# Moving the zero fills from GpSimd's DMA queue to SyncE's, and the loads and stores the other way

One core of one Trainium2 chip. The metric is the device time of one execution in microseconds; medians of several executions are quoted.

## The reference

The outputs are one forward value and eight gradients of a block made of one query's attention and a gated feed-forward layer, all bf16.

```python
# x: (1,1,448); k_cache, v_cache: (1, 8, 32768, 256); wq: (448, 4096); wo: (4096, 448)
# w_gate, w_up: (448, 1792); w_down: (1792, 448)
W = 4096                                     # only the last 4096 of 32768 keys are used
q = (layernorm(x) @ wq)                      # 16 heads of 256, two for each of 8 key heads
p = softmax(q @ k_cache[:, :, Sk-W:].T / 16)
h = x + (p @ v_cache[:, :, Sk-W:]) @ wo
g, u = layernorm(h) @ w_gate, layernorm(h) @ w_up
out = h + (g * u) @ w_down
# returned: out and the gradients by x, k_cache, v_cache, wq, wo, w_gate, w_up, w_down
```

What matters here is the size of two of the gradients. Those by `k_cache` and `v_cache` have 134 MB each, and seven eighths of each are zero, because only the last 4096 rows of a head are used. So 235 MB of zeros have to be written, out of 335 MB that the kernel moves.

## The kernel before

A zero tile of 128 rows by 16 KB in on-chip memory is the source of nearly all fills. One fill writes it to 2 MB of `out_2` or `out_3` in 128 rows. Its upper half is lent to feed-forward weights for a while, so there are three groups: 42 full fills, 13 that read the lower half twice ("half fills", rows of 8 KB), and, once VectorE has zeroed the upper half again, 48 more full ones. Five late jobs write the last 18.9 MB from another region.

```python
LD = nc.sync                                 # loads and stores
ZQ = nc.gpsimd                               # zero fills
HALF0, HALF1 = 42, 55
...
LD.dma_start(out=wqA, in_=wq_A)              # query weights, 3.67 MB in two pieces
LD.dma_start(out=wqB, in_=wq_B)
LD.dma_start(out=x_bf[:], in_=A_x.rearrange("a b d -> (a b) d"))
...
def send_fills(n0, n1, halves=False):
    for reg in fills[n0:n1]:
        if halves:                           # L131
            ZQ.dma_start(out=reg.rearrange("p (k f) -> p k f", k=2), in_=zeros[:, 0:ZW // 2].unsqueeze(1).to_broadcast([128, 2, ZW // 2]))
        else:                                # L133
            ZQ.dma_start(out=reg, in_=zeros)

send_fills(0, HALF0)
send_fills(HALF0, HALF1, True)
...
load_kv(K_off[0], A_k_cache, 0)              # L197: a head's keys or values, 2 MB
LD.dma_start(out=dh2_bc[:], in_=grad_out.rearrange("a b d -> (a b) d").to_broadcast([128, D]))   # L200
...
if n == 1:                                   # in the feed-forward backward
    nc.vector.memset(ar(ZW // 2, ZW // 2), 0.0)      # L433: the second zeroing
    send_fills(HALF1, len(fills))
...
LD.dma_start(out=wq2A, in_=wq_A)             # L461: the query weights once more
LD.dma_start(out=wq2B, in_=wq_B)             # L462
...
for o, g, n0, n1, f in late_jobs:            # L663: 18.9 MB of zeros
    reg = zero_rows(o, g, n0, n1, f)
    for i in range(reg.shape[0]):
        LD.dma_start(out=reg[i], in_=ar(2 * ZW - f, f))
```

The source order is not the order of issue: a scheduler sorts the instructions of each engine when the program is built, and on one queue they are then issued strictly in that order. SyncE's and ScalarE's transfers go over what the profile calls the hardware path, GpSimd's over the software path.

Of the kernel before, what the change touches and what calls it, by code (L numbers as in the profile page):

```python
# [24 lines left out]
EPS = 1e-5  # L25
SCALE = 1.0 / 16.0
ZW = 8192
HALF0, HALF1 = 42, 55
NZ = (Sk - W) * Dh // (128 * ZW)
KB = 512  # L30

# [2 lines left out]
def kernel(  # L34
        ctx, tc, A_x, A_k_cache, A_v_cache, A_wq, A_wo, B_x, B_w_gate, B_w_up, B_w_down, grad_out,
           out_0, out_1, out_2, out_3, out_4, out_5, out_6, out_7, out_8):
    nc = tc.nc
    LD = nc.sync
    ZQ = nc.gpsimd

    const = ctx.enter_context(tc.tile_pool(name="const", bufs=1))
    small = ctx.enter_context(tc.tile_pool(name="small", bufs=2))
# [11 lines left out]
    def ar(off, n):  # L54
        return arena[:, off:off + n]

    def kv_at(off):
        return ar(off, T * Dh).rearrange("p (t d) -> p t d", d=Dh)
# [6 lines left out]
    wqA = ar(MB, 24 * KB).rearrange("p (c j) -> p c j", c=3)  # L65
    wqB = ar(MB + 24 * KB, 4 * KB)
# [29 lines left out]
    x_bf = const.tile([1, D], bf16)  # L96
    dh2_bc = const.tile([128, D], bf16)
    wq_A = A_wq[0:384, :].rearrange("(c p) j -> p c j", c=3)
    wq_B = A_wq[384:D, :].rearrange("r (h j) -> (r h) j", h=2)
    LD.dma_start(out=wqA, in_=wq_A)  # L100
    LD.dma_start(out=wqB, in_=wq_B)
    LD.dma_start(out=x_bf[:], in_=A_x.rearrange("a b d -> (a b) d"))

    ident_bf = const.tile([128, 128], bf16)
    make_identity(nc, ident_bf[:])
# [9 lines left out]
    def zero_rows(o, g, n0, n1, f):  # L115
        reg = o[0, g, 0:Sk - W, :].rearrange("s d -> (s d)")[n0 * 128 * ZW:n1 * 128 * ZW]
        return reg.rearrange("(n p f) -> n p f", p=128, f=f)
# [3 lines left out]
    for g in range(G):  # L121
        for o in (out_2, out_3):
            if g == G - 1 and o is out_3:
                continue
            reg = zero_rows(o, g, 0, 5 if g == G - 1 else NZ, ZW)
            fills += [reg[i] for i in range(reg.shape[0])]
# [8 lines that stand above are left out]
# [61 lines left out]
    def load_kv(off, cache, g):  # L196
        LD.dma_start(out=kv_at(off), in_=cache[0, g, Sk - W:, :].rearrange("(p t) d -> p t d", t=T))  # L197

    load_kv(K_off[0], A_k_cache, 0)
    LD.dma_start(out=dh2_bc[:], in_=grad_out.rearrange("a b d -> (a b) d").to_broadcast([128, D]))  # L200
    load_kv(V_off[0], A_v_cache, 0)
# [61 lines left out]
    with tc.tile_pool(name="ps_m", bufs=1, space=bass.MemoryType.PSUM) as ps_m, \  # L263
# [61 lines left out]
        def load_wo(n):  # L325
            LD.dma_start(out=wo_sb[:, 16 * n:16 * n + 16, :], in_=A_wo.rearrange("(p j) n -> p j n", j=32)[:, 16 * n:16 * n + 16, :])

# [18 lines left out]
    def block_views(n):  # L346
        f0, nb = BLOCKS[n]
        w = 128 * nb
        wgu = ar(wgu_off[n % 2], 8 * w).rearrange("p (c i f) -> p c i f", c=4, i=2)
        wd = ar(wd_off[n % 2], nb * D).rearrange("p (b n) -> p b n", n=D)  # L350
        return f0, nb, w, wgu, wd

    def load_block(n):
        f0, nb, w, wgu, wd = block_views(n)
        for eng, i, wt in ((LD, 0, B_w_gate), (nc.scalar, 1, B_w_up)):
            eng.dma_start(out=wgu[:, 0:3, i, :], in_=wt[0:384, :].rearrange("(c p) f -> p c f", c=3)[:, :, f0:f0 + w])
            eng.dma_start(out=wgu[0:DQ, 3, i, :], in_=wt[384:D, f0:f0 + w])
        LD.dma_start(out=wd, in_=B_w_down[f0:f0 + w, :].rearrange("(p b) n -> p b n", b=nb))

    load_block(0)  # L360
    load_block(1)

    with tc.tile_pool(name="ps_mid", bufs=3, space=bass.MemoryType.PSUM) as ps_mid, \
# [34 lines left out]
        for n in range(len(BLOCKS)):  # L398
# [31 lines left out]
            if n + 2 < len(BLOCKS):  # L430
                load_block(n + 2)
# [63 lines left out]
    with tc.tile_pool(name="work2", bufs=2) as work2, tc.tile_pool(name="lnw", bufs=1) as lnw, \  # L495
# [164 lines left out]
        for o, g, n0, n1, f in late_jobs:  # L660
            reg = zero_rows(o, g, n0, n1, f)
            for i in range(reg.shape[0]):
                LD.dma_start(out=reg[i], in_=ar(2 * ZW - f, f))  # L663

# [1 line left out]
_INS = ['A_x', 'A_k_cache', 'A_v_cache', 'A_wq', 'A_wo', 'B_x', 'B_w_gate', 'B_w_up', 'B_w_down', 'grad_out']  # L666
# [26 lines left out]
```

## Time and profile before

| | before |
|---|---|
| time, median (range) of 4 runs | 798.87 us (798.55 to 799.08) |
| span of the profiled run | 797.2 us |
| bytes moved, mean rate | 334.76 MB, 420 GB/s |
| busy: TensorE, VectorE, ScalarE | 60%, 55%, 25% |
| 334.76 MB at 431 GB/s (the good slices) | 776.7 us |

Whatever the kernel takes beyond 776.7 us is time in which the 16 DMA engines were not all at work at their best. In any stretch of the span it is (431 - rate) x length / 431.

### The profile page before, as it was taken

How to read it: one execution, taken by the hardware profiler on the slowest of the kernel's cores; microseconds unless marked ns; L12 is line 12 of the kernel's file. 1: busy time of each engine (PE TensorE's matmuls, PEld its weight loads, DVE VectorE, ACT ScalarE, POOL GpSimd, SP SyncE). 2: the span in 40 equal slices, each digit the busy share in tenths (PEclk: the TensorE clock that was granted, in tenths of full speed). 3: DMA queues.
4: the chain of work that ended last, by engine and by line, in shares of the span. 5: the costliest groups of instructions: out<-in, count | busy, mean ns of one | idle time of the engine just before them, and what ended most of it. 6: DMA issues, size and time to landing. Idle time of an engine off the chain costs nothing.

```text
span 797.2 us, 7318 instructions
## 1 busy us (share of the span) xinstructions
PE 478.9 (60%) x2926; PEld 222.6 (28%) x2926; DVE 437.1 (55%) x629; ACT 196.0 (25%) x309; POOL 61.8 (8%) x112
## 2 busy tenths in 40 slices
PE   0459999999999999251409478684450553722000
PEld 0334434344344333121208334331220211310000
DVE  2116584765846782263690679579653784964000
ACT  0142314134132201010102126353330442534000
POOL 4000000010101111100210001010000000000000
PEclk9989999999999999555558779766555556765555
DMA  9999999999999999999999999999999999999995
GB/s 349 431 430 430 428 431 430 430 428 430 430 423 427 427 419 413 423 421 424 432 428 423 424 431 431 428 425 427 424 424 422 424 424 424 423 427 418 433 434 247
DMA packets 29352, 334.76 MB, mean 420 GB/s; under 512 B 2819, under 2 KB 5894, under 8 KB 7814
## 3 DMA queue, kind: packets, MB, share of 16 engines
q0 software_dynamic: 16496, 216.01, 64.0%
q1 hardware_dynamic: 11382, 116.68, 34.8%
q10 hardware_dynamic: 1440, 1.61, 0.6%
q8 instruction: 23, 0.38, 0.2%
q14 instruction: 11, 0.09, 0.0%
HBM read 53.69 MB, written 280.59 MB: 419 GB/s over the span
## 4 chain that ended last, share of the span: by engine, by line
PE 37%; DMA 32%; DVE 16%; ACT 4%; issue 2%; another core or an unknown queue 0%; SPq 0%; DVEq 0%; ACTq 0%
DMA out_dram<-arena 19%; PE M_ps L317 12%; PE ok_ps L320 7%; PE rows_ps L256 6%; PE tr_ps L253 4%; DMA dh_bc<-in_grad_out_dram 4%; DMA arena<-in_A_k_cache_dram 4%; DMA arena<-in_B_w_down_dram 3%; ACT arena L270 2%; DVE arena L635 2%; DVE arena L459 2%; PE dqb_ps L502 2%; DMA arena<-in_B_w_gate_dram 2%; DVE arena L650 2%; PE d_ps L643 2%
## 5 line engine op out<-in xcount | busy, mean ns | idle before, releaser
L312 DVE TENSOR_TENSOR arena<-arena,p_f 128x2048 bf16<-128x2048 bf16 x64 | 145.4, 2286 | 61.6 <-PE M_ps L317 61.5
L317 PE MATMUL M_ps<-arena 128*128 128x512 bf16 x512 | 128.9, 380 | 0.2 <-ACT arena L323 0.2
L643 PE MATMUL d_ps<-arena,rT 32*128 32x512 bf16 x256 | 46.6, 529 | 111.0 <-DVE arena L651 63.9
L253 PE MATMUL tr_ps<-ident_bf,arena 128*128 128x128 bf16 x1024 | 92.5, 242 | 19.6 <-ACT arena L611 11.2
L256 PE MATMUL rows_ps<-arena,vpad 128*16 128x512 bf16 x256 | 90.6, 451 | 19.9 <-DVE arena L613 14.6
L133 POOL DMA_DIRECT2D out_dram<-arena x90 | 48.6, 542 | 538.5 <-DMA out_dram<-arena 491.3
L253 PEld LDWEIGHTS <-arena 128*128 128x128 bf16 x1024 | 69.0, 108 | 73.8 <-issue 64.4
L270 ACT COPY arena<-tr_ps 128x1024 bf16<-128x1024 bf16 x64 | 61.8, 1015 | 64.7 <-PE tr_ps L253 64.7
L647 ACT CAST arena<-d_ps 128x512 bf16<-128x512 f32 x64 | 37.7, 589 | 128.4 <-PE d_ps L643 128.3
L320 PE MATMUL ok_ps<-arena 128*16 128x512 bf16 x256 | 63.8, 381 | 0.9 <-DVE arena L297 0.9
L317 PEld LDWEIGHTS <-arena 128*128 128x128 bf16 x512 | 43.3, 99 | 59.0 <-issue 23.2
L611 ACT COPY arena<-tr_ps 128x1024 bf16<-128x1024 bf16 x32 | 32.6, 1019 | 94.6 <-PE tr_ps L253 36.4
L650 DVE CAST arena<-d_ps 128x512 bf16<-128x512 f32 x64 | 43.8, 684 | 16.9 <-PE d_ps L643 16.4
L651 DVE CAST arena<-d_ps 128x512 bf16<-128x512 f32 x64 | 43.5, 679 | 11.2 <-DMA out_dram<-arena 11.2
L643 PEld LDWEIGHTS <-rT 32*128 32x128 bf16 x256 | 11.2, 96 | 136.5 <-issue 90.0
L648 ACT CAST arena<-d_ps 128x512 bf16<-128x512 f32 x64 | 38.1, 595 | 11.9 <-DMA out_dram<-arena 11.9
L635 DVE TENSOR_TENSOR arena<-R_sb,tl_f 128x4096 bf16<-128x4096 bf16 x8 | 35.4, 4419 | 0.7 <-ACT R_sb L633 0.7
L256 PEld LDWEIGHTS <-vpad 128*16 128x16 bf16 x256 | 19.1, 92 | 58.4 <-issue 51.3
L320 PEld LDWEIGHTS <-arena 128*16 128x16 bf16 x256 | 19.1, 89 | 41.6 <-issue 20.5
L514 DVE CUSTOM_DVE_ANT_0 arena<-arena 128x4096 bf16<-128x4096 bf16 x3 | 13.1, 4423 | 23.9 <-ACT arena L507 23.9
L285 ACT ACTIVATE e_f<-cols_ps,nbias 128x32 f32<-128x32 f32 x16 | 4.5, 286 | 86.8 <-DVE nbias L281 86.8
L258 DVE COPY arena<-rows_ps 16x512 f32<-16x512 f32 x16 | 10.8, 676 | 26.6 <-PE rows_ps L256 26.6
(198 smaller groups left out, 387.9 us busy)
## 6 DMA issues: line engine op xcount, KB each, us to landing
out_dram<-arena POOLq DMA_DIRECT2D x103, 2048.0 KB, 51.7
out_dram<-arena SPq DMA_DIRECT2D x18, 2048.0 KB, 32.3
arena<-in_A_v_cache_dram SPq DMA_DIRECT2D x10, 2048.0 KB, 50.0
arena<-in_A_k_cache_dram SPq DMA_DIRECT2D x8, 2048.0 KB, 29.2
out_dram<-arena SPq DMA_DIRECT2D x4, 4096.0 KB, 43.8
arena<-in_A_wq_dram SPq DMA_DIRECT2D x2, 3072.0 KB, 20.6
arena<-in_A_wo_dram SPq DMA_DIRECT2D x2, 1792.0 KB, 14.5
out_dram<-arena SPq DMA_DIRECT2D x2, 1792.0 KB, 15.1
```

The costliest lines, as they stand in the source:

```text
L133: ZQ.dma_start(out=reg, in_=zeros)
L253: nc.tensor.transpose(tr_ps[:, dh, i, :], X_sb[:, 4 * q + i, dh * 128:(dh + 1) * 128], ident_bf[:])
L256: nc.tensor.matmul(rows_ps[:], lhsT=pad[:, dh, 16 * q:16 * q + 16], rhs=XT[:, dh].rearrange("p t k -> p (t k)"), start=(q == 0 and dh == 0 ...
L270: sT_ps = dots(kv_at(K_off[g]), KT_slot, vpad[g % 2], rows1, ps_c, "cols", lambda q, XT, ps: nc.scalar.copy(out=XT, in_=ps))
L312: nc.vector.tensor_tensor(out=pK, in0=K_sb[:, 4 * c:4 * c + 4, :].unsqueeze(2).to_broadcast([128, 4, 2, Dh]), in1=p_f[:, c::8, :].unsqueez ...
L317: nc.tensor.matmul(M_ps[:, vh, :], lhsT=V_sb[:, t, vh * 128:(vh + 1) * 128], rhs=pK[:, i, :, :].rearrange("p h d -> p (h d)"), start=(t == ...
L320: nc.tensor.matmul(ok_ps[:].rearrange("p k d -> p (k d)"), lhsT=ppad[g % 2][:, 8 * (t % 4) + t // 4, :], rhs=both(g, t), start=(g == 0 and ...
L635: nc.vector.tensor_tensor(out=RB_, in0=R_sb[:].unsqueeze(1).to_broadcast([128, 8, 512]), in1=tl_f[:].unsqueeze(2).to_broadcast([128, 8, 51 ...
L643: nc.tensor.matmul(d_ps[:, qi].rearrange("p w d -> p (w d)"), lhsT=rT[32 * q:32 * (q + 1), :], rhs=RB_[32 * q:32 * (q + 1), l, :], start=T ...
L648: nc.scalar.copy(out=stK[:, t:t + 2, :], in_=d_ps[:, :, 1, :])
L650: nc.vector.tensor_copy(out=stV[:, t:t + 2, :], in_=d_ps[:, :, 0, :])
L651: nc.vector.tensor_copy(out=stK[:, t:t + 2, :], in_=d_ps[:, :, 1, :])
```

## The change

The intent: SyncE, which computes nothing, issues the long row of fills, and GpSimd no longer spends time writing their descriptors. The query weights' first load stays at the head of the queue that is ready first. HALF1 goes from 55 to 61 so that the fills last until the second zeroing.

```diff
-HALF0, HALF1 = 42, 55
+HALF0, HALF1 = 42, 61
...
-    LD = nc.sync
-    ZQ = nc.gpsimd
+    LD = nc.gpsimd
+    ZQ = nc.sync
...
-    LD.dma_start(out=wqA, in_=wq_A)
-    LD.dma_start(out=wqB, in_=wq_B)
-    LD.dma_start(out=x_bf[:], in_=A_x.rearrange("a b d -> (a b) d"))
+    ZQ.dma_start(out=wqA, in_=wq_A)
+    ZQ.dma_start(out=wqB, in_=wq_B)
+    ZQ.dma_start(out=x_bf[:], in_=A_x.rearrange("a b d -> (a b) d"))
...
-        for eng, i, wt in ((LD, 0, B_w_gate), (nc.scalar, 1, B_w_up)):
+        for eng, i, wt in ((LD, 0, B_w_gate), (LD, 1, B_w_up)):
...
             for i in range(reg.shape[0]):        # the late jobs
-                LD.dma_start(out=reg[i], in_=ar(2 * ZW - f, f))
+                ZQ.dma_start(out=reg[i], in_=ar(2 * ZW - f, f))
```

## The prediction

> **What bounds the kernel now.** I read the DMA rows of the page first, because a program that zero-fills most of two large gradients can hardly be bound by anything else, then the stretches of the span, the end of the span, and last the waits of the issuing engines.
>
> ```profile
> DMA  9999999999999999999999999999999999999995
> GB/s 349 431 430 430 428 431 430 430 428 430 430 423 427 427 419 413 423 421 424 432 428 423 424 431 431 428 425 427 424 424 422 424 424 424 423 427 418 433 434 247
> DMA packets 29352, 334.76 MB, mean 420 GB/s; under 512 B 2819, under 2 KB 5894, under 8 KB 7814
> ...
> q0 software_dynamic: 16496, 216.01, 64.0%
> q1 hardware_dynamic: 11382, 116.68, 34.8%
> q10 hardware_dynamic: 1440, 1.61, 0.6%
> ```
>
> The 16 DMA engines are at 90% or more in 39 of 40 slices, at 413 to 434 GB/s in 38 of them. Only the first and last slice fall short. q0 is the GpSimd queue, and 216 MB is exactly 103 fills of 2 MB; q1 is SyncE's (loads, stores, and 18.9 MB of late zero fills), q10 ScalarE's (the up-projection weights). So 334.76 MB at the 431 GB/s of the good slices would take 777 us of the 797.2 us span: 20 us is all there is to gain. The stretches split it:
>
> ```profile
> 0.00:5.00 5.00, 0.00 (x0) 0.00 (x0) 3.00 (x11) 1.28 (x1) 4.43 (x9) 1.00 0.62 208
> 5.00:10.00 5.00, 0.37 (x1) 0.09 (x1) 1.54 (x7) 0.00 (x0) 4.44 (x9) 1.00 1.01 336
> 10.00:20.00 10.00, 0.00 (x0) 0.00 (x0) 0.00 (x0) 0.00 (x0) 0.53 (x1) 1.00 1.02 429
> 20.00:180.00 160.00, 139.30 (x911) 61.68 (x911) 83.06 (x93) 45.92 (x64) 10.13 (x19) 0.97 1.01 430
> ...
> 735.00:785.00 50.00, 0.00 (x0) 0.00 (x0) 0.00 (x0) 0.00 (x0) 0.00 (x0) 0.50 1.01 430
> 785.00:790.00 5.00, 0.00 (x0) 0.00 (x0) 0.00 (x0) 0.00 (x0) 0.00 (x0) 0.50 0.67 288
> 790.00:797.20 7.20, 0.00 (x0) 0.00 (x0) 0.00 (x0) 0.00 (x0) 0.00 (x0) 0.50 0.08 34
> ```
>
> The last two columns are DMA share and GB/s. In the first 10 us the DMA misses (431-208) x 5 + (431-336) x 5 = 1.59 MB, worth 3.7 us. At the end, from 735 us nothing computes at all (all five engine columns are 0.00), the DMA runs on alone, and in the last 12.2 us it misses 5 x (431-288) + 7.2 x (431-34) = 3.57 MB, worth 8.3 us. There 34 GB/s at a share of 0.08 of 16 is one or two DMA engines still working when the others are done: the 16 do not finish together. The rest of the 20 us, some 8 us, is the slices at 413 to 428.
>
> Two more views say that the computing engines are not the bound.
>
> ```profile
> POOL out_dram L133 <- DMA out_dram<-arena: 491.3, 75, 9.6
> POOL out_dram L131 <- DMA out_dram<-arena: 76.4, 13, 9.3
> POOL out_dram L133 <- DVE arena L433: 35.6, 1, 35.6
> ```
>
> GpSimd, while it issues the fills, waits 568 us for an earlier fill to finish (it issues 8, then one whenever one lands), so a backlog of fills always stands behind the DMA. The one wait on computing, 35.6 us for VectorE's second zeroing of the half of the zero tile that weights had used, did not let the DMA run dry: the slices there are 413 to 423. And the chain that ended last shows VectorE and TensorE between stores, but its last piece is the DMA. A change of schedule inside the span is therefore worth nothing unless it makes the DMA idle.
>
> **What the Trainium skill says.** "DMA: Bandwidth & Descriptors", section "Issuing engines are not separate DMA queues": all issuers run on the same 16 engines and interleave; issuing from another saves only issue time. The trace agrees: the rate is the same 430 GB/s with both queues working (20 to 180 us) as with SyncE's alone (735 to 785 us). The same page, "Queues, rings and completion order": each engine takes turns between its queues by packet. The trace agrees: from 60 to 160 us, where both queues hold 16 KB rows, they move some 215 GB/s each, and a queue with small rows gets one small row for each 16 KB fill. The same page, "Latency and other measured facts": engines 7 and 15 are usually slower, its best guess being the descriptor rings that only GpSimd's software path uses. The trace does not number the engines, but one or two stragglers at the end fit; no run yet shows the cause. "SBUF — State Buffer", section "SBUF: two separate sides": VectorE in its two-port modes can keep GpSimd from writing descriptors. In this trace GpSimd's issues of full fills took 533 ns in the median and 1,101 ns at most, with VectorE 55% busy, so I count no loss for it.
>
> **The change, part by part.** No byte is added or removed; all engines' work is the same, except that ScalarE loses its six weight-load issues. The order of instructions shows SyncE with 3 loads, 103 fills and the 5 late fills, GpSimd with every other load and store.
>
> *Start.* The first query weights (3.67 MB) still go first on SyncE, so bytes begin at about 2 us as before. The fills now stand behind these weights, and the first key block comes on GpSimd's queue at about 5 us instead of a fill. Before, x landed at 21 us, the first keys at 31 us, and the broadcast of grad_out, whose small rows alternated with 16 KB fills, at 36 us; TensorE was busy 20.9 us of the 40 us from 20 to 60 us, and 245.8 of 248 us after that. I expect keys and grad_out to be down when x is, so the attention stage starts some 10 to 15 us earlier. The DMA was full anyway, so the end gains nothing from this. The dip to 336 GB/s at 5 to 10 us, where GpSimd wrote 8 fills' descriptors, may shrink: -1 us.
>
> *Feed-forward weights.* Gate and up had a queue each beside the fills; now they follow each other on one queue. For a block of 640 columns each DMA engine gets 28 + 28 + 8 rows. Beside half fills (8 KB rows, some 0.31 us each) that is 64 turns of some 0.36 us = 23 us, against (28 + 8) turns of some 0.43 us = 15 us. So about 8 us later for blocks 0 and 2, 16 us together (block 1 hides under block 0's computing), which eats the gain of the start. The second zeroing, at 375.8 us before, stays within some 15 us of that. Do the fills last till then? By then loads are some 46 MB. 61 fills are 128 MB; 174 MB at 425 GB/s last to 411 us. The old 55 (115 MB) would have lasted to 381 us. So the six more half fills are cover, and the margin is some 20 us or more: 0 us.
>
> *Steady stretches.* Fills on the other queue. The stretch of SyncE alone at the end ran at 430; fills alone on q0 (slices around 180, 280 and 480 us) at 425 to 432. I give 0.3% of the 500 us of mixed work: -1.5 us.
>
> *End.* Before, 18.9 MB of late fills lay between SyncE's last stores, and one of those waits was 42 us. Now the stores compete with fills only by turns, so computing ends somewhat before its old 732 us, perhaps at 715. SyncE's fills (234 MB in all) then run alone to the end, and the zero tile they need is written (at 667 us before) long before. GpSimd's last stores would have to slip by about 40 us to stick out. The stragglers remain; if their lag grows with descriptors on the software path, it shrinks from 16,496 to about 11,500 of them (12,822 on the hardware queues now, less some 560 of the first weights and 720 of the late fills), 30% of 8.3 us: -2.5 us, with a good chance of 0.
>
> Sum: -1 - 1.5 - 2.5 = -5 us; I add back 1 us for small holes while waits rearrange. 799 - 4 = 795 us.
>
> **The rivals.** (1) The fill queue runs dry: SyncE waits for the second zeroing or for GpSimd's loads while the stores are not yet there. For it: the weights' loads get slower, and the issuer order is strict on one queue. Against it: 20 us of cover. Each us beyond it costs at most half a us to one; a 40 us miss would make some 815. (2) Loads become the bound through the software path: VectorE blocks descriptors, stages of attention stretch, and stores stick out at the end. For it: VectorE is 55% busy. Against it: 533 ns issues, and 40 us of slack at the end. It would have to stretch by more than 40 us; 810 to 830. (3) The stragglers are wholly the software path's and vanish, with the start hole halved: 8.3 + 2 + 1.5 us, 787. (4) The DMA does not care who issues: 799.
>
> **Range and chances.** Rivals 3 and 4 frame the likely ground: 787 to 799 us, widened to 786 to 804 us for a little more gain and for short dry spells. Faster by over 2% means below 783 us, which leaves 6 us above the 777 us of pure transfer, less than the start alone costs with its 2 us of empty DMA and a tail: 3%. Slower by over 2% needs rivals 1 or 2 in force: 5%. Within 2%: 92%.
>
> **What would show each step right or wrong.** The DMA row still 9 in 39 slices and the queue rows swapped to about 238 MB hardware and 97 MB software; x, keys and grad_out landing by about 20 us; the wait of the 62nd fill on the second zeroing absent or shorter than the 8 fills in flight; computing over before 735 us; and in the last 12 us the hole of 3.57 MB smaller. I am wrong if the DMA row shows slices under 9 in the middle, if the rate of the steady slices moves by over 1%, or if GpSimd's stores, not SyncE's fills, end the span.

## More of the kernel before

In the built program each path uses eight completion semaphores in turn, so a path has at most eight transfers under way, and the next one waits for the eighth before it. SyncE and ScalarE share the eight of the hardware path.

## The result, and the profile after

The changed kernel takes 799.73 us (median of 4 runs, 799.66 to 800.42). The kernel before took 798.87 us in the same rounds. The ratio is 1.0013, with a 95% interval from 0.9996 to 1.003: the same time. (Ratios here are the mean time of one kernel's fast runs over the mean of the other's of the same rounds, so not quite the ratio of the medians quoted.) The gain of 4 us did not come; if anything there is a loss of 1 us.

First the page of the kernel after, the DMA rows and the queues.

```profile
DMA  9999999999999999999999999999999999999996
GB/s 340 430 430 428 429 431 430 430 429 427 428 430 428 424 419 422 424 424 426 426 403 417 428 427 430 429 429 424 425 424 423 425 424 418 418 423 430 436 427 269
DMA packets 27396, 334.76 MB, mean 420 GB/s; under 512 B 2881, under 2 KB 2882, under 8 KB 5090
...
q1 hardware_dynamic: 18530, 238.56, 70.8%
q0 software_dynamic: 8832, 95.74, 28.6%
```

The queues have changed places: 238.56 MB now go over the hardware path, 95.74 MB over the software path. The DMA row is 9 in 39 slices as before, and the mean rate is the same 420 GB/s. Packets on the software path fell to 8,832; the prediction had some 11,500, because it did not know that this path joins short rows into longer packets.

Next SyncE's issues in the kernel after (start, length, line, transfer, count), and what SyncE waited for (total us, times, longest).

```profile
4.28 258.61 SPq L133 DMA_DIRECT2D out_dram<-arena  x42
267.54 121.83 SPq L131 DMA_DIRECT2D out_dram<-arena  x19
389.62 299.50 SPq L133 DMA_DIRECT2D out_dram<-arena  x42
695.75 33.63 SPq L663 DMA_DIRECT2D out_dram<-arena  x5
```

```profile
SPq L133 <- DMA out_dram<-arena: 494.7, 71, 10.5
SPq L131 <- DMA out_dram<-arena: 18.3, 4, 6.5
SPq L133 <- DMA arena<-in_A_wq_dram: 11.9, 2, 6.1
```

The fills follow each other without a gap. SyncE waits only for an earlier transfer to land, which is what a queue with a backlog does; no wait on the second zeroing (L433) is left. That zeroing was done at 361.7 us, and the 62nd fill, the first to need it, was issued at 389.6 us. Rival 1, the dry queue, did not happen.

Then the stretches of the kernel after (start:end, length, busy time of five engines, TensorE's clock, DMA share, GB/s).

```profile
0.00:5.00 5.00, 0.00 (x0) 0.00 (x0) 3.00 (x11) 1.28 (x1) 4.43 (x9) 1.00 0.63 203
5.00:10.00 5.00, 0.37 (x1) 0.09 (x1) 1.54 (x7) 0.00 (x0) 2.90 (x6) 1.00 1.03 434
10.00:20.00 10.00, 0.42 (x4) 0.26 (x4) 0.52 (x2) 0.00 (x0) 0.00 (x0) 1.00 1.00 363
15.00:18.00 3.00, 0.00 (x0) 0.00 (x0) 0.00 (x0) 0.00 (x0) 0.00 (x0) 1.00 0.89 179
20.00:180.00 160.00, 152.71 (x998) 67.68 (x999) 90.24 (x102) 51.44 (x74) 5.26 (x10) 0.98 1.01 429
376.00:465.00 89.00, 51.13 (x303) 35.98 (x304) 55.19 (x132) 13.59 (x19) 2.90 (x5) 0.71 1.01 420
402.00:406.00 4.00, 3.56 (x14) 2.57 (x15) 2.12 (x14) 0.82 (x1) 0.00 (x0) 0.50 1.00 328
735.00:785.00 50.00, 0.00 (x0) 0.00 (x0) 0.00 (x0) 0.00 (x0) 0.00 (x0) 0.50 1.01 433
785.00:790.00 5.00, 0.00 (x0) 0.00 (x0) 0.00 (x0) 0.00 (x0) 0.00 (x0) 0.50 0.82 351
790.00:797.90 7.90, 0.00 (x0) 0.00 (x0) 0.00 (x0) 0.00 (x0) 0.00 (x0) 0.50 0.16 68
```

And the same view of the kernel before, for the stretches that the prediction did not show.

```profile
7.00:10.00 3.00, 0.00 (x0) 0.00 (x0) 0.00 (x0) 0.00 (x0) 2.44 (x5) 1.00 0.99 268
15.00:18.00 3.00, 0.00 (x0) 0.00 (x0) 0.00 (x0) 0.00 (x0) 0.14 (x1) 1.00 1.04 441
376.00:465.00 89.00, 42.90 (x223) 32.08 (x223) 55.49 (x135) 9.32 (x15) 10.63 (x20) 0.63 1.01 427
402.00:406.00 4.00, 0.00 (x0) 0.00 (x0) 4.00 (x15) 0.00 (x0) 0.00 (x0) 0.50 0.98 418
```

Three things are to be seen. The hole of before at 5 to 10 us (336 GB/s, with its bottom of 268 at 7 to 10 us) is gone: 434. In its place there is one at 15 to 18 us, 179 GB/s where before had 441. And the stretch from 376 to 465 us lost 7 GB/s, most of it in a dip at 402 to 406 us. The end is a little better: 351 and 68 GB/s, where before had 288 and 34.

As time lost against 431 GB/s:

| stretch | before | after | forecast of the change |
|---|---|---|---|
| first 20 us | 3.7 | 4.2 | -1 |
| 20 to 785 us (the remainder) | 8.5 | 9.4 | -1.5 |
| after 785 us | 8.3 | 7.6 | -2.5 |
| all: span - 776.7 us | 20.5 | 21.2 | -5, with 1 added back: -4 |

The computing side moved as forecast and was worth nothing. x landed at 19.5 us instead of 21.1, the broadcast of grad_out at 18.8 instead of 36. TensorE was busy 270.7 of the 280 us from 20 to 300 us, where it had been 258.7. The last computing instruction ended at 710 us instead of 732. The end of the span is set by the fills, and these take what the DMA takes.

### The profile page after: what moved, and what is told of

Its sections match the earlier page's. It is cut to its first block, busy times and chain, and to the rows that moved or that the text cites. A ratio compares the mean times of both kernels' runs of the same rounds, so it can differ in the third digit from the quotient of the medians.

```text
span 797.9 us, 7310 instructions
## 1 busy us (share of the span) xinstructions
PE 474.3 (59%) x2926; PEld 220.5 (28%) x2926; DVE 436.6 (55%) x629; ACT 195.7 (25%) x309; POOL 44.3 (6%) x77
## 3 DMA queue, kind: packets, MB, share of 16 engines
q1 hardware_dynamic: 18530, 238.56, 70.8%
q0 software_dynamic: 8832, 95.74, 28.6%
## 4 chain that ended last, share of the span: by engine, by line
PE 41%; DMA 22%; DVE 15%; issue 6%; ACT 4%; POOL 0%; DVEq 0%; SPq 0%; POOLq 0%; ACTq 0%
DMA out_dram<-arena 15%; PE M_ps L317 13%; PE ok_ps L320 8%; PE rows_ps L256 6%; PE tr_ps L253 5%; ACT arena L270 3%; DMA arena<-in_B_w_down_dram 3%; DMA x_bf<-in_A_x_dram 2%; DVE arena L459 2%; PE dqb_ps L502 2%; DVE arena L650 2%; PE d_ps L643 2%; DMA arena<-in_B_w_up_dram 1%; DVE arena L651 1%; DVE arena L428 1%
## 5 line engine op out<-in xcount | busy, mean ns | idle before, releaser
L256 PEld LDWEIGHTS <-vpad 128*16 128x16 bf16 x256 | 18.9, 91 | 57.5 <-issue 49.8
L320 PEld LDWEIGHTS <-arena 128*16 128x16 bf16 x256 | 19.1, 89 | 41.6 <-issue 20.5
L613 DVE COPY arena<-tr_ps 128x1024 bf16<-128x1024 bf16 x32 | 21.7, 683 | 3.3 <-PE tr_ps L253 2.3
```

Of the source, the lines that this page charges most:

```text
L256: nc.tensor.matmul(rows_ps[:], lhsT=pad[:, dh, 16 * q:16 * q + 16], rhs=XT[:, dh].rearrange("p t k -> p (t k)"), start=(q == 0 and dh == 0 ...
L320: nc.tensor.matmul(ok_ps[:].rearrange("p k d -> p (k d)"), lhsT=ppad[g % 2][:, 8 * (t % 4) + t // 4, :], rhs=both(g, t), start=(g == 0 and ...
```

## The experiments

Sixteen kernels ran. Four questions led them: what the new holes at 15 us and 404 us are, whether they decide anything, what the software path costs at all, and why its cost does not show in the whole kernel. Unless said otherwise the edit is to the changed kernel, the result was correct, and "before" is the kernel before in the same rounds. Its medians were 798.8 to 799.2 us.

### grad_out's broadcast moved to SyncE

```diff
-    LD.dma_start(out=dh2_bc[:], in_=grad_out. ... .to_broadcast([128, D]))
+    ZQ.dma_start(out=dh2_bc[:], in_=grad_out. ... .to_broadcast([128, D]))
```

> The changed kernel with one load moved: the broadcast of grad_out to 128 partitions goes on SyncE's queue (after x, before the first fill) instead of GpSimd's. In the changed kernel the DMA moved 179 GB/s from 15 to 18 us, where that broadcast ran on GpSimd's queue in packets of 4480 bytes that took 1.26 us each. Theory A (the merged broadcast packets make the hole): the hole of 15 to 18 us is gone, no second with under 300 GB/s in the first 20 us after the ramp, and the time falls by some 1.5 us, to 798.2. Rival (the hole is the onset of the first fills, whichever load is beside it): a hole of 2 to 3 us stays where the first fill starts, and the time stays at 799.7.

Measured: 1033.79 us against 798.79, ratio 1.294. Below: SyncE's issue of this load, VectorE's wait for it, and one of the stretches.

```profile
331.54 4.96 SPq L200 DMA_DIRECT2D dh_bc<-in_grad_out_dram  x1
DVE pad L213 <- DMA dh_bc<-in_grad_out_dram: 289.4, 1, 289.4
72.00:262.00 190.00, 0.00 (x0) 0.00 (x0) 0.00 (x0) 0.00 (x0) 0.00 (x0) 0.50 1.01 431
```

Although it stands early in the source, the scheduler put this load behind all 61 fills of the first two groups. It was issued at 331.5 us and landed at 359.7 us. Until then the computing engines stood still from about 70 us on (the stretch shows 0.00 in each) while the fills ran at 431 GB/s. (The expectation of the later run on ScalarE names another wait instead, GpSimd's 233 us for the first 42 fills. The trace has that one too, but it ended at 263 us; the wait for the broadcast ended last.) When the fills had run out, the second zeroing was still far off: SyncE waited 308 us for it, and the DMA fell to 0 to 164 GB/s. So this run does show what breaks such a kernel, but it was no test of the hole at 15 us. One thing holds: without the broadcast most of that hole was gone, with 367 GB/s from 15 to 18 us and 304 GB/s from 18 to 20 us.

### The second load of the query weights on ScalarE

```diff
-        LD.dma_start(out=wq2A, in_=wq_A)
-        LD.dma_start(out=wq2B, in_=wq_B)
+        nc.scalar.dma_start(out=wq2A, in_=wq_A)
+        nc.scalar.dma_start(out=wq2B, in_=wq_B)
```

> The changed kernel with the second load of the query weights issued by ScalarE (hardware path) instead of GpSimd. In the changed kernel the fills' packets slow down from 309 to 410 to 452 ns for 4 us after GpSimd issued this load (402 to 406 us, 328 GB/s). Theory B (the software path's start-up with this load makes the dip, about 1 us): the dip is gone and the time falls by some 1 us to 798.7. Rival (any reads that join fills running alone cost this much): a dip of the same size where the load begins, time 799.7. If both A and B hold, the two holes explain why the change did not gain what was predicted at the start and in the steady stretches.

Measured: 805.24 us, ratio 1.0079. SyncE's wait and the stretch that it emptied:

```profile
SPq L131 <- DMA arena<-in_A_wq_dram: 37.5, 1, 37.5
390.00:399.00 9.00, 0.00 (x0) 0.00 (x0) 9.00 (x35) 0.00 (x0) 0.00 (x0) 0.50 0.23 88
```

A fill waited 37.5 us for a weight load that ScalarE had not yet issued. The two engines share the eight semaphores of the hardware path: the fill's turn came behind the load's, and the load waited for VectorE. For 9 us the DMA had a fifth of its rate. The experiment broke the kernel by a new wait and says nothing on the dip at 404 us.

### 55 instead of 61 fills ahead of the second zeroing

```diff
-HALF0, HALF1 = 42, 61
+HALF0, HALF1 = 42, 55
```

> The changed kernel with 55 instead of 61 fills ahead of the second zeroing, as in the kernel before. In the changed kernel the zeroing was done at 361.7 us and SyncE reached its 62nd fill only at 389.6 us without any wait, so the six more fills bought nothing. Theory: same time within 0.5 us (799.7), no wait on the second zeroing longer than the fills in flight. Rival (the fills would have run dry): a hole in the DMA row near 360 us and 803 or more.

Measured: 799.39 us (799.16 to 799.85), ratio 1.0008 with an interval from 0.9996 to 1.0021. The six extra half fills buy nothing. Between 376 and 465 us the rate was 425 GB/s instead of 420, worth 1.0 us; the loss after 785 us was 8.3 us instead of 7.6. Little of the gain in the middle reached the end.

### No software path at all

```diff
-    LD = nc.gpsimd
+    LD = nc.scalar
```

> The changed kernel with GpSimd's loads and stores moved to ScalarE's queue, so that no descriptor goes through GpSimd's software path. It decides what makes the 16 DMA engines finish apart. If the software path's descriptors make stragglers (rival 3 of the prediction), the hole of the last 12 us shrinks from 7.0 us of full rate to under 4 and the time falls to some 794 to 796, unless ScalarE, which now computes and issues in one order, delays loads so much that the DMA runs dry. If stragglers come from elsewhere, the hole stays at 6 to 9 us and the time at 797 to 802. Holes A and B should be gone in either case (about 2.5 us).

Measured: 812.34 us, ratio 1.0167. The shared semaphores again:

```profile
SPq L133 <- DMA arena<-in_A_wq_dram: 47.7, 2, 35.4
```

SyncE's fills stopped behind ScalarE's loads that waited for buffers, and slices in the middle fell to 307 to 350 GB/s. In the last 12.2 us the DMA ran at 333 GB/s, a loss of 2.8 us instead of some 8, and the 16 engines ended 1.3 us apart. That would fit the idea that the stragglers belong to the software path; but the engines can catch up with each other in a dry spell, and the last deep one was at 560 to 580 us (317 GB/s). Two runs that kept the software path had a dry spell too, and their engines ended further apart: 6.3 us in the broadcast's run on SyncE, some 380 us after it, and 3.9 us in the run with the weights on ScalarE, some 400 us after it. The software path may have a part in it, then, but the times since the dry spell differ, so this does not decide.

### grad_out's broadcast on ScalarE

```diff
-    LD.dma_start(out=dh2_bc[:], in_=grad_out. ... .to_broadcast([128, D]))
+    nc.scalar.dma_start(out=dh2_bc[:], in_=grad_out. ... .to_broadcast([128, D]))
```

> The changed kernel with the broadcast of grad_out issued by ScalarE as its first instruction. The earlier try, on SyncE's queue, took 1033 us, because the scheduler then put the weights of block 1 ahead of key block 3 in GpSimd's order, where they waited 233 us for the first 42 fills; this time the order of GpSimd and SyncE is otherwise unchanged. Theory A (the broadcast in merged packets on the software path makes the hole of 15 to 18 us, 179 GB/s): the hole shrinks by at least half, the loss of the first 20 us (4.5 us of full rate in the changed kernel) falls to under 3.5, the time falls by about 1 us to 798.7. Rival (the onset of the fills makes the hole): 4.5 us lost as before, 799.7.

Measured: 800.19 us (799.47 to 800.39) against 799.10, ratio 1.0012. Here the load was issued early and all else kept its order. The hole at 15 to 18 us was gone (10 to 20 us: 428 GB/s), and it came back elsewhere: the first 5 us had 93 GB/s instead of 203, with a hole at 2 to 4 us, where the small rows now lay among the first query weights. The first 20 us lost 4.0 us instead of 4.2. So the hole at 15 us is the broadcast's. It is 128 times the same 896 bytes. On the software path of the changed kernel the trace has it as merged packets, the larger of 4,480 bytes or five rows; all 16 engines began theirs between 15.8 and 16.7 us and ended them between 17.1 and 17.7 us, 1.26 us each on average: they stood still together. On ScalarE's path the rows stayed single and made a hole all the same, 120 ns each on average. In the kernel before they came in turns with 16 KB rows, nearly all of them from 29 to 35 us, and took 41 ns each, while the rate was 429 GB/s. So merging is not what the two holes share. In both, the broadcast's neighbours were rows of the first query weights; in the kernel before they were mostly fills.

### The fills alone, on GpSimd and on SyncE

Both kernels zero the tile and issue 112 fills of 2 MB (235 MB), nothing else. The result is wrong, as the other outputs are not written.

```diff
+    ZQ = nc.gpsimd            # the first kernel; nc.sync in the second
+    zeros = const.tile([128, ZW], bf16)
+    nc.vector.memset(zeros[:], 0.0)
+    for o in (out_2, out_3):
+        for g in range(G):
+            reg = o[0, g, 0:Sk - W, :]. ... ("(n p f) -> n p f", p=128, f=ZW)
+            for i in range(reg.shape[0]):
+                ZQ.dma_start(out=reg[i], in_=zeros[:])
```

> Wrong result on purpose: only the zero fills, all 112 of 2 MB (234.9 MB), all on GpSimd's queue, nothing else in the program. It measures by itself what the prediction guessed at for the steady stretches (-1.5 us) and the end (-2.5 us). Theory D (the DMA does not care who issues): 548 to 556 us, mean packet of 16 KB within 0.3% of that of the twin on SyncE, hole of the last 12 us the same within 1.5 us. Rival (the software path slows the fills and makes stragglers): slower than the twin by 1.5 us or more, with a hole at the end that is larger by 2 us or more.

> Wrong result on purpose: the twin, all 112 fills on SyncE's queue. Theory D: same time as on GpSimd's queue within 1 us, and the engines finish as far apart. Rival: 1.5 us or more faster, with a small hole at the end. If the engines finish together in both twins, the stragglers of the full kernels come from the mixture of queues and not from either path.

Measured: 574.58 us on GpSimd, 559.49 us on SyncE, each within 0.1 us in four runs. Alone, the software path does cost: 15.1 us, or 2.7%. The stretches (here with VectorE and GpSimd as the only engines), first GpSimd's kernel, then SyncE's:

```profile
10.00:555.00 545.00, 0.00 (x0) 55.43 (x104) 1.00 1.01 422
560.00:572.80 12.80, 0.00 (x0) 0.00 (x0) 1.00 0.26 113
```

```profile
10.00:545.00 535.00, 0.00 (x0) 0.00 (x0) 1.00 1.01 427
545.00:557.70 12.70, 0.00 (x0) 0.00 (x0) 1.00 0.87 372
```

Steady rate 422 against 427, and a long tail at a quarter of the rate. The trace's packet records split the 15.1 us. A 16 KB packet takes 623.5 ns on average against 616.9; 14,336 of them on 16 engines make 5.9 us. On GpSimd's path eight of the engines end some 8 us after the other eight, which is worth about 4 us (they fall behind bit by bit: 0.4 us at the first fill, 3 us at the 35th); on SyncE's path all 16 end within 0.4 us. The span goes on for 5.6 us after the last packet against 1.2 us: 4.4 us. The start takes about 0.7 us longer. Sum: 15.0 us.

### Only the late fills moved

The kernel before, with its 18.9 MB of late fills on GpSimd's queue as well:

```diff
-                LD.dma_start(out=reg[i], in_=ar(2 * ZW - f, f))
+                ZQ.dma_start(out=reg[i], in_=ar(2 * ZW - f, f))
```

> The kernel before with one part of the change alone: the 5 late fills (18.9 MB) behind the other fills on GpSimd's queue instead of between SyncE's last stores. The computing engines should finish near 710 us instead of 732 us, since the last stores no longer stand behind late fills. Theory (nothing that finishes earlier counts while the DMA is full): time unchanged within 1 us of 798.8. Rival (the last stores are on the path that sets the end): 5 us or more faster.

Measured: 798.45 us against 799.10, ratio 0.9992 (0.9978 to 1.0006). The time did not move, as it should not where the fills set the end. Computing, though, ended at 725 us, so the forecast end of 710 us was wrong for this kernel: the late fills alone account for some 7 of the 22 us by which computing ended earlier in the changed kernel.

### The fills alone, with the engines set apart

One idea on the difference between 623 and 617 ns was that 16 engines in step with each other get in each other's way, and that the path matters only through the step it keeps. Fifteen short loads of 1, 2, ... 15 rows of 4 KB on SyncE ahead of the fills give the engines different starts. These two kernels, and the next of fills alone, have a wrong result as well.

```diff
+    stagger = const.tile([16, 15 * 2048], bf16)
+    for k in range(1, 16):
+        nc.sync.dma_start(out=stagger[0:k, (k - 1) * 2048:k * 2048], in_=A_wq[0:k, 0:2048])
```

> Wrong result on purpose. The program of fills alone on GpSimd's queue, with 15 small loads (4 KB rows on the first k of the 16 DMA engines, k = 1 to 15, on SyncE's queue) that put the engines out of step by some 0.16 us each at the start. In step, fills alone took 623 ns per packet on GpSimd's queue and 617 ns on SyncE's (574.6 and 559.5 us), while in the full kernels, where the engines are out of step, fills running alone take 613 ns on either. Theory E (engines in step get in each other's way, and the software path suffers more): out of step, packets fall to 611 to 615 ns and the gap between the twins to under 6 us (555 to 561 us here). Rival (the software path is slower by itself, and in the full kernel the loads hide it): 570 to 576 us as before, 620 ns or more.

> Wrong result on purpose. The same on SyncE's queue. Theory E: packets of 611 to 614 ns, 554 to 557 us. Rival: 617 ns and 559 to 561 us as before.

Measured: 574.68 us on GpSimd and 561.09 us on SyncE; packets 622.8 and 616.6 ns. By these totals the idea fails. But the stagger did not last. The small packets that report an engine's share of a fill as done show it: on SyncE the 16 engines were 1.5 us apart at the first fill, 0.3 us at about the 28th, and 0.3 us at the last, no more than without the stagger; on GpSimd they began 1.7 us apart. While they were apart, the packets were shorter (mean of the 16 KB packets that started in the stretch):

| fills alone | early stretch | early, in step | early, staggered | 200 to 500 us, first kernel | 200 to 500 us, staggered one |
|---|---|---|---|---|---|
| on SyncE | 15 to 45 us | 616.9 ns | 613.2 ns | 616.8 ns | 616.9 ns |
| on GpSimd | 15 to 30 us | 624.4 ns | 614.2 ns | 623.3 ns | 623.4 ns |

So as long as the engines are out of step, a packet takes about the 613 ns of the whole kernel on SyncE's path, and nearly that on GpSimd's. One profile of each kernel shows this; a stagger that lasts was not tried.

### grad_out's broadcast behind the first four loads

```diff
     load_kv(K_off[0], A_k_cache, 0)
-    LD.dma_start(out=dh2_bc[:], in_=grad_out. ... .to_broadcast([128, D]))
     load_kv(V_off[0], A_v_cache, 0)
     load_kv(K_off[1], A_k_cache, 1)
     load_kv(V_off[1], A_v_cache, 1)
+    LD.dma_start(out=dh2_bc[:], in_=grad_out. ... .to_broadcast([128, D]))
```

> The changed kernel with the broadcast of grad_out issued by GpSimd behind the second key and value blocks instead of behind the first key block, so that its packets alternate with 16 KB fills, as its rows did in the kernel before. On ScalarE it had merely moved the hole to 2 to 4 us (800.2 us). Theory A2 (the broadcast costs DMA time only where nothing large stands beside it): the hole of 15 to 18 us is gone or under 0.6 us, no new one appears, the loss of the first 20 us falls from 4.5 us to some 3.3, and the time is 798.5 to 799.7, since part of a gain of 1 us can again be lost at the end, where the slowest of the 16 engines decides. Rival (the onset of the fills makes the hole): loss of 4.2 us or more in the first 20 us.

Measured: 800.44 us (799.12 to 800.84) against 798.78, ratio 1.0017. The first 20 us ran at 361 GB/s instead of 341 and lost 3.2 us instead of 4.2, as the idea wanted. The merged packets of 4,480 bytes, now at 44 to 47 us in turns with fills, took 0.17 us each instead of 1.26, although 11 of the 16 began within 0.3 us: neither merging nor the software path makes them slow by itself. The time got no better: in the profiled run, which was this kernel's slowest, 8.9 us were lost after 785 us instead of 7.6, and 10.3 instead of 9.4 in between. A hole of 1 us at the start is not what decides the end.

### The fills alone, alternately on both queues

```diff
-                ZQ.dma_start(out=reg[i], in_=zeros[:])
+                (nc.sync, nc.gpsimd)[n % 2].dma_start(out=reg[i], in_=zeros[:]); n += 1
```

> Wrong result on purpose. Fills alone again, 112 of them, one on SyncE's queue and the next on GpSimd's in turn. It links the twins (559.5 us on SyncE, 574.6 us on GpSimd) to the full kernels, in which moving 216 MB of fills from one path to the other changed nothing. Theory F (the software path costs only when it has the DMA to itself): 556 to 562 us, the engines finish within 2 us of each other. Rival (each DMA on the software path costs its share wherever it runs): about half way, 565 to 569 us, with half of the engines some 4 us late at the end.

Measured: 566.75 us, against 559.49 for all on SyncE and 574.58 for all on GpSimd (another call): half of the fills on the software path cost half of the difference, 7.3 of 15.1 us. Half of the engines ended some 4 us late. So neither a busy hardware queue beside it nor the mixture as such takes the cost away.

### Twice as many transfers, in packets half as long

If the cost is one per transfer or per packet, more of them on one path should show it. The full fills behind the second zeroing were cut into two halves of each row: 48 fills into 96 in the kernel before (on GpSimd), 42 into 84 in the changed kernel (on SyncE).

```diff
-                ZQ.dma_start(out=reg, in_=zeros)
+                for c in ((0, ZW // 2), (ZW // 2, ZW)) if n0 >= HALF1 else ((0, ZW),):
+                    ZQ.dma_start(out=reg[:, c[0]:c[1]], in_=zeros[:, c[0]:c[1]])
```

> The kernel before with the 48 fills after the second zeroing cut into 96 of 1 MB (two halves of each row, so 8 KB packets), all on GpSimd's queue; the order of instructions is otherwise the same. It doubles the suspected cost: fills alone cost 0.135 us per fill more on GpSimd's queue than on SyncE's (15.1 us in 112; 7.3 us in 56). Theory G (that cost is paid in the full kernel too): the time rises by 4 to 6.5 us more than in the twin on SyncE. Rival H (in the full kernel nobody waits for it): it rises by as much as the twin, within 1 us; smaller packets alone may cost both some 2 us.

> The twin: the changed kernel with the 42 fills after the second zeroing cut in the same way into 84, on SyncE's queue. Theory G: 799.7 us plus at most 2 us for the smaller packets. Rival H: the same rise as on GpSimd's queue, within 1 us.

Measured: 806.98 us on GpSimd, ratio 1.0103, and 802.84 us on SyncE, ratio 1.0054, against 798.79. That is 8.2 us over the kernel before and 3.1 us over the changed kernel's 799.73 (from its own rounds, on another chip), so some 5 us more on the software path (with 48 fills cut instead of 42). A stretch in which only 8 KB fill packets ran, first on GpSimd, then on SyncE:

```profile
771.00:785.00 14.00, 0.00 (x0) 0.00 (x0) 0.00 (x0) 0.00 (x0) 2.66 (x5) 0.50 1.01 411
```

```profile
700.00:735.00 35.00, 0.00 (x0) 0.00 (x0) 0.00 (x0) 0.00 (x0) 0.00 (x0) 0.50 1.01 419
```

GpSimd's queue now ended last. From 771 us on it ran alone, at 411 GB/s with packets of 322 ns; SyncE alone moved the same packets at 419 GB/s, 315 ns each. The closing after the last packet was 3.4 us against 1.7. So part of the software path's cost appears where it works alone and ends the program; where the rest of the 5 us lies was not sought. In the kernel before it did not end the program: SyncE's late fills did.

### Half as many transfers of the same packets

```diff
+            if not halves and todo and todo[0][0] is par:      # the next fill lies behind this one
+                todo.pop(0); ZQ.dma_start(out=par[i:i + 2]. ... ("n p f -> p n f"),
+                                          in_=zeros.unsqueeze(1).to_broadcast([128, 2, ZW]))
```

Fills joined in pairs to 4 MB, in the kernel before (103 fills in 65 transfers) and in the changed kernel (the 84 full ones in 48).

> The kernel before with its full fills joined in pairs to 4 MB where two follow each other in one tensor (7 fills become 4 transfers), the source named twice by a zero step; same bytes, same 16 KB packets, same order of instructions on all engines. GpSimd issues 65 transfers instead of 103. Cutting 48 fills in two cost 8.1 us on GpSimd's queue and 3.1 us on SyncE's. Theory G (a cost of 0.05 to 0.13 us for every transfer on the software path, paid in the full kernel too): 2 to 5 us faster, 794 to 797 us, which would beat both kernels. Rival H (the cost goes with packets and bytes, not with transfers, or is not paid here): within 1 us of 798.8.

> The twin: the changed kernel with its full fills joined in the same way on SyncE's queue (84 become 48). Theory G: within 1 us of 799.7, since a transfer on the hardware path costs next to nothing by itself. Rival: a gain as large as on GpSimd's queue, which would be the gain of fewer transfers on any path.

Measured: 798.50 us (798.21 to 798.75), ratio 0.9992 with an interval from 0.998 to 1.0005, and 800.53 us, ratio 1.0017, against 798.91. The number of transfers costs nothing that shows, on either path. No version beats the kernel before clearly. Of the eight correct kernels whose fills kept their row size and never stopped, the three with the fills on GpSimd took 798.5 to 799.2 us and the five with the fills on SyncE 799.4 to 800.5 (medians); two of the five are slower than the kernel before with an interval clear of 1. A small loss by the change is likelier than a gain.

## Why the prediction was right and wrong

**Right: the bound, and what does not count.** The kernel is bound by the DMA; the bytes are the same; the queues changed places; the attention stage started earlier, computing ended 22 us earlier (of which the prediction's reason, the late fills, explains some 7), and that was worth nothing. The fills never ran dry. The second zeroing came 28 us before its fill; it began at 359.9 us, 16 us earlier than before, so the slower weight loads did not eat up the earlier start as the prediction had it. Time within 2%, and inside the range. Rival 4, "The DMA does not care who issues: 799", is what happened.

**Wrong: the sum.** "Sum: -1 - 1.5 - 2.5 = -5 us" was made of three small gains, and none came as forecast. The step that failed is the pricing: it took for granted that the fills' path costs DMA time that a move would save, and in the whole kernel the three terms measured +0.5, +0.9 and -0.7 us.

*Start, forecast -1, profile +0.5.* The step said that the dip "where GpSimd wrote 8 fills' descriptors, may shrink". It vanished. What the step left out is that the broadcast of grad_out now comes beside the last rows of the query weights, before any fill, in merged packets that took 1.26 us each. That opened the hole at 15 to 18 us. That the broadcast makes this hole is shown by taking it away (the run on ScalarE) and by moving it (the run behind four loads). What makes it slow are its neighbours and not its path, as far as the packets' times in these runs go: beside weight loads 1.26 us for a merged packet of five rows and 120 ns for a single row, beside fills 0.17 us and 41 ns. Why is not shown. A smaller dip at 18 to 20 us stayed where the broadcast came later (304 and 328 GB/s) and is not explained.

*Steady stretches, forecast -1.5, profile about +0.9.* The step compared 430 GB/s on SyncE with "425 to 432" on GpSimd and took 0.3% from that, though 430 lies inside that range. The trace's packet records could have told: 16 KB rows of the fills took 617.4 ns on average on GpSimd before and 617.7 ns on SyncE after, and about 613 ns on either where only fills were running. The stretch from 20 to 180 us agrees: 430 GB/s before, 429 after. (The 430 and 433 GB/s at the end say nothing of the path, as SyncE issued those fills in both kernels.) There was no path difference to gain. The kernels of fills alone do have one (623.5 against 616.9 ns), so a measurement of fills by themselves would have misled here. The staggered kernels suggest why: alone, the engines run in step; out of step they took 613 to 614 ns on either path.

The dip at 402 to 406 us, about 1 us of this term, is not settled. It comes 2 to 10 us after the second load of the query weights is issued in the changed kernel and in the five variants that leave that load on GpSimd with the other loads (55 fills, the broadcast on ScalarE or behind four loads, split and joined fills on SyncE); windows of 4 us fall to 324 to 348 GB/s and follow the issue when it shifts from 398 to 403 us. That looked like the software path's doing. But the kernels before with joined and with split fills have SyncE issue this load and dip to 336 and 342 GB/s all the same, while the kernel before itself and the one with moved late fills do not. The experiment meant for it failed.

*End, forecast -2.5, profile -0.7.* The step was "if their lag grows with descriptors on the software path, it shrinks ... 30% of 8.3 us". The packets on the software path fell by more than that, from 16,496 to 8,832, and the end went from 8.3 to 7.6 us; with the same 8,832 the run with 55 fills has 8.3 us. So the lag is not proportional to the software path's packets in this kernel. The last packets of the 16 engines ended between 785.9 and 795.6 us before, with two stragglers, and between 786.8 and 796.5 us after, with one.

*Two readings* in the prediction's working are off without consequence. From 60 to 160 us the queues moved 234 and 195 GB/s, not 215 each. And the slices in which GpSimd waited for the second zeroing, 342 to 378 us, have 421 and 424 GB/s, not 413 to 423.

**Where the expected gain went.** The account of eight kernels, each from one profile, us lost against 431 GB/s:

| kernel | first 20 us | in between | after 785 us | all |
|---|---|---|---|---|
| before | 3.7 | 8.5 | 8.3 | 20.5 |
| before, late fills on GpSimd | 3.6 | 9.0 | 7.4 | 20.0 |
| before, joined fills | 3.9 | 9.3 | 6.8 | 20.0 |
| after | 4.2 | 9.4 | 7.6 | 21.2 |
| after, 55 fills | 4.2 | 8.4 | 8.3 | 20.9 |
| after, broadcast on ScalarE | 4.0 | 9.8 | 7.2 | 21.0 |
| after, broadcast behind loads | 3.2 | 10.3 | 8.9 | 22.4 |
| after, joined fills | 4.2 | 9.6 | 8.5 | 22.3 |

The parts move by up to 2 us from kernel to kernel, and the sum by 2.4 us. In some kernels a part that gets better is paid for by another (55 fills: 1.0 us less in between, 0.7 us more at the end), in others no part gets better (joined fills) or more is lost than gained (broadcast behind loads), so these sums do not show that the parts repay each other. That they do would fit a span that ends when the last of 16 engines ends: a hole that holds back an engine which is ahead costs nothing, and one that lets them catch up with each other is repaid at the end. No run of its own shows it. The runs of one kernel lie up to 1.7 us apart, too (799.12 to 800.84), so a forecast of gains of 1 to 2.5 us each from one profile had no ground.

**What stays open.** Why packets are longer when the engines run in step (617 and 623 ns against 613), and whether that is all of the difference between fills alone and the whole kernel; why eight of the 16 engines lag on the software path; how much the software path has to do with the stragglers of the whole kernel; what makes the dip near 404 us.

## What to carry to other kernels

Where all DMA engines are busy from start to end, moving transfers between queues moves computing but not the time: look for bytes to save, or holes to close, and account for them against the best rate in the same trace before promising a gain. A load that moves to a queue with a long backlog may land behind all of it, whatever its place in the source (here 290 us of waiting for 896 bytes), and queues that share completion semaphores stop each other; so check the order of issue after any such move. A cost measured with one kind of transfer alone need not appear in the whole program, and a gain read from rates that overlap is none.

## What the Trainium skill lacked or had wrong

- "DMA: Bandwidth & Descriptors", section "Issuing engines are not separate DMA queues", says that issuing from several engines at once saves only issue time; it has no figure for what the issuing path costs a long row of transfers. In the whole kernel moving the fills saved nothing (799.7 against 798.9 us). For fills alone it makes 2.7%, 574.6 us from GpSimd and 559.5 us from SyncE, of which the steady packets make 5.9 us, the lag of eight engines some 4 us, and the closing after the last packet 4.4 us.
- The same page, section "Latency and other measured facts", names engines 7 and 15 as the usual slow ones and takes the software path's descriptor rings as its best guess. With fills on the software path alone, eight of the 16 engines lagged, by some 8 us (the trace does not number them); with SyncE alone all ended within 0.4 us. In the whole kernel stragglers remain when the fills are on SyncE (7.6 us lost at the end, 8.3 before), so there they are not the software path's fills.
- The same page, section "SWDGE vs HWDGE vs iDMA", says that a packet may hold several descriptors, preferably up to 4096 bytes, but not what becomes of a broadcast: rows of 896 bytes became packets of up to 4,480 bytes. Nor has a page how much a broadcast's time hangs on its neighbours: such a packet took 1.26 us beside weight loads, with the DMA at 179 GB/s for 3 us, and 0.17 us beside fills.
- No page has it that the programs built here let SyncE and ScalarE take turns at the same eight completion semaphores. A fill waited 37.5 us for a load that ScalarE had not issued (805.2 us instead of 799.7).
